# Retention and a gated FFN in one kernel: gates by seven products in tile 2, a relative state, whole-array products and a new order

## The chip, the cores and the metric

The kernel runs on one core of a Trainium2 chip. A core has five engines that run their own instruction streams and meet through semaphores: TensorE (PE, with its weight loads shown apart as PEld), VectorE (DVE), ScalarE (ACT), GpSimd (POOL) and SyncE (SP), which only issues transfers. TensorE writes into PSUM, which has eight banks of 128 x 512 float32; DVE and ACT read them, POOL does not. The metric is the device time of one execution in microseconds (us), as a median of several.

## The reference

```python
def _attn_ref(q, k, v):                     # 4 batches, 8 heads, 768 tokens, 64 wide
    gamma = 1.0 - 2.0 ** (-5.0 - np.arange(H))
    for t in range(S):
        state = gamma * state + einsum('bhd,bhe->bhde', k[:, :, t], v[:, :, t])
        y[:, :, t] = scale * einsum('bhd,bhde->bhe', q[:, :, t], state)

def _moe_ref(x, w_gate, w_val, w_out):      # 3072 tokens, 512 wide, 1536 hidden
    gate = 1.0 / (1.0 + np.exp(-(x @ w_gate)))
    val = x @ w_val
    return gate * val @ w_out
```

The output y of the first part, with the heads side by side, is x of the second. Inputs and output are float32 in memory; the kernel multiplies in bfloat16.

## The kernel before

**Tiles.** The 768 tokens are cut into six chunks of 128. A tile t is one chunk of all four batches: 512 tokens of the FFN. Its attention is done in two "pairs" P = 2t, 2t + 1 of two batches c each. Attention is chunked: scores of a chunk with itself (`scores`, L216) are masked with the decay (`mask`, L221) and multiplied by v (`intra`, L239); what came before enters through a state per head: `inter` (L233) multiplies q by the block-diagonal copy `zbd` of the state, `state` (L261) makes k v of the chunk, with k scaled by the decay (`scaled`, L206 or L209), `state_sum` (L270) adds it to `za`, and `state_out` (L274) copies `za` into `zbd`. `y_out` (L254) scales y by a table `taby` and leaves it transposed in `xT`.

The decay is handled absolutely: k of tile t is divided by gamma to the power of its own token number, and y of tile t is multiplied by gamma to the power of that number. So each tile t > 0 has its own two masks (`tile_tables`, L152, on POOL) and its own table for y (L157, on POOL), and the state is a plain sum.

**FFN.** Gates and values are products of `xT` with `wg` and `wv`, in twelve blocks of 128 hidden units. Direct blocks are made by `up` (512 columns a matmul) or `up_half` (256). Others go by a scheme of seven products in place of eight (`half_product`) on two blocks of units and two halves of the tokens, which needs sums of weights (`halves_sums`, L340, into `ws`) and of inputs (`x_sums`, L350, into `xs`), made once, and evictions with additions afterwards: `gate_copy`, `gate_add`, `gate_sigmoid` (L409, L414, L419) for gates, `val_copy`, `val_add`, `val_finish` (L388, L393, L399 to L404) for values. A direct gate block is one sigmoid (`up_sigmoid`, L308), a direct value block one product of it with the gate (`up_finish`, L311). The output product goes the same way (`product`, with `hidden_sums`, L453, and `weight_sums`, L435), then `fast_copy`, `fast_add` (L489, L494) and `fast_store`. `halves_sums` and `hidden_sums` can be done on DVE or on POOL.

In tile 2 the values go by seven products and the gates are direct; in tiles 3 and 4 both go by seven, in tile 5 both but the gates of the first two blocks.

**Matmuls.** `mm` (L282 to L288) issues a product either whole (L284, a 128 x 128 stationary operand) or as two column halves of 64 (L288), by the flag `whole`. Scores use half the rows and all columns (64 x 128). All results of TensorE but the state's go to one pool `ff` of seven PSUM banks, one bank a call of `bank`. A new tenant of a bank waits until DVE or ACT has read the old one.

**Order.** After a prologue that fills the pipeline and issues the loads of weights and of the first pairs, everything is issued from a list `ORDER` of six strings (L662 to L733), one for each tile, on a manual schedule: each engine runs its instructions in the order in which the strings name the steps. A step is two letters and a number: `gm`, `vm` direct gate and value products, `sg`, `mu` their evictions, `ag` to `bm` the same by halves, `gp`, `gc`, `ga`, `gs` the gate's seven-product steps, `vp`, `vc`, `va`, `vf`, `vd` the value's (vd: finish on DVE), `dp`, `dc`, `da`, `ds` the output's, `ad`, `dd` weight sums on DVE and `aw`, `dw` on POOL, `hs` hidden sums on DVE and `hg` on POOL, `xs`, `xg` input sums, `wp`, `wc` output weights, `tt` tables, `kt`, `sc`, `mk`, `in`, `ia`, `yo`, `sm`, `zs`, `zo` the attention, `lk`, `lq`, `lv` loads of k, q and v issued by POOL, and `xk`, `xq` transposing loads issued by SP. A + or - moves the step to the next or the last tile. A step in capitals sets `whole`; the order before has none.

Of the kernel before, what the change touches and what calls it, by code (L numbers as in the profile page):

```python
# [17 lines left out]
def kernel(  # L18
# [14 lines left out]
    C = 128  # L33
# [17 lines left out]


# [7 lines left out]
    def load(P, *what):  # L60
        for n in what:
            held, x = {"k": (kn, k), "q": (qn, q), "v": (vn, v)}[n]
            held[P] = ld.tile([C, 2 * H, D], BF16, tag=n, name=n + "n", bufs=4)
            nc.gpsimd.dma_start(out=held[P], in_=src(x, P))

    def load_one(P, c, *what):
        for n in what:
            held, x = {"k": (kn, k), "q": (qn, q), "v": (vn, v)}[n]
            if P not in held:
                held[P] = ld.tile([C, 2 * H, D], BF16, tag=n, name=n + "n", bufs=4)  # L70
# [24 lines left out]
    for n, x, eng in (("k", k, nc.sync), ("q", q, nc.sync)):  # L95
        raw[n] = ffn.tile([C, H, D], F32, tag="ob", name="raw", bufs=4)
        eng.dma_start(out=raw[n], in_=x[0, :, 0:C, :].rearrange("h s d -> s h d"))
    early = ffn.tile([128, 4, 128], F32, tag="gs", name="early", bufs=6)
# [24 lines left out]
    nc.vector.tensor_scalar(toky, dist, tok[:, 0:1], None, op0=ALU.add)  # L123
    nc.vector.tensor_tensor(dist, dist, past, op=ALU.add)
    first = const.tile([128, NT], F32, name="first")
    nc.vector.tensor_scalar(first, tok, tok[:, 0:1], None, op0=ALU.subtract)
    mask0 = at.tile([128, 2, NP, C], F32, tag="maskd", name="mask0")
# [5 lines left out]
    tabk = const.tile([128, NT, H], F32, name="tabk")  # L133
    tabz = const.tile([128, NT, NP], F32, name="tabz")
    taby0 = const.tile([128, NP, C], F32, name="taby0")
    maskd, taby = {}, {}
# [11 lines left out]
    def tile_tables(t, i):  # L148
        if i < 2:
            if t not in maskd:  # L150
                maskd[t] = at.tile([128, 2, NP, C], F32, tag="maskd", name="maskd")
            nc.gpsimd.affine_select(maskd[t][:, i], tabk[:, t, i:H:2].unsqueeze(2).to_broadcast([128, NP, C]),  # L152
                                    pattern=[[0, NP], [1, C]], base=0, channel_multiplier=-1,
                                    compare_op=ALU.is_ge, fill=0.0)
            return
        taby[t] = at.tile([128, NP, C], F32, tag="taby", name="taby", bufs=1)
        nc.gpsimd.tensor_tensor(taby[t], taby0, tabz[:, t, :].unsqueeze(2).to_broadcast([128, NP, C]), op=ALU.mult)  # L157
# [5 lines left out]
    def bank(shape, dt=F32):  # L163
        return pf.tile(shape, dt, tag="ff", name="ff", padded_shape=[128, 2 * NP, C] if dt == BF16 else None)

    def new_qkT(P):
        qkT[P] = ld.tile([128, 2, 2, NP, C], BF16, tag="qkT", name="qkT", bufs=4)
# [32 lines left out]
    def scaled(P, h):  # L200
        x = kn[P].rearrange("s (c h) d -> s c h d", c=2)
        if P not in kt:
            kt[P] = ld.tile([C, 2 * H, D], BF16, tag="kt", name="kt", bufs=2)
        to = kt[P].rearrange("s (c h) d -> s c h d", c=2)
        if P < 4:
            nc.vector.tensor_tensor(to, x, tabk[:, P // 2, :].unsqueeze(1).unsqueeze(3).to_broadcast([C, 2, H, D]),  # L206
                                    op=ALU.mult)
        else:
            nc.scalar.activation(to[:, :, h, :], x[:, :, h, :], AX.Copy, scale=tabk[:, P // 2, h:h + 1])  # L209
# [9 lines left out]
    def mask(P, c, i):  # L219
        st[P, c, i] = at.tile([128, NP, C], BF16, tag="st", name="st", bufs=8)  # L220
        nc.vector.tensor_tensor(st[P, c, i], sc[P, c][i], (mask0 if P < 2 else maskd[P // 2])[:, i], op=ALU.mult)  # L221
# [5 lines left out]
    def inter(P, c):  # L227
        y[P, c] = bank([128, NP, C])
        if P > 1:
            for p in range(NP):  # L230
                for i in range(2):
                    half = slice(i * D, (i + 1) * D)
                    nc.tensor.matmul(y[P, c][half, p, :], zbd[P % 2][:, c, p, half], qkT[P][:, 1, c, p, :],  # L233
                                     start=(p == 0), stop=False, skip_group_check=True)
# [7 lines left out]
    def y_out(P, c, eng="a"):  # L242
        t = P // 2
        if t not in xT:
            xT[t] = at.tile([128, NP, 512], BF16, tag="xT", name="xT")
# [7 lines left out]
        else:  # L253
            nc.vector.tensor_tensor(o, y[P, c], taby[t], op=ALU.mult)  # L254
# [9 lines left out]
    def state_sum(P):  # L264
# [4 lines left out]
        else:  # L269
            nc.vector.tensor_tensor(za[j], za[j], zz[P], op=ALU.add)  # L270
# [11 lines left out]
    def mm(during, o, left, right, **kw):  # L282
# [9 lines left out]
    def hidden(t):  # L292
        if t not in hT:
            hT[t] = ffn.tile([128, NFF, 512], BF16, tag="hT", name="hT", bufs=2)
        return hT[t]

    def up(t, n1, which, lo=0, hi=512):
# [3 lines left out]
        for kk in range(KT):  # L301
            mm(t, us[t, n1, which][:, lo:hi], w[:, kk, n1 * 128:(n1 + 1) * 128], xT[t][:, kk, lo:hi],
               start=(kk == 0), stop=(kk == KT - 1))

    def up_sigmoid(t, n1, lo=0, hi=512):
        if (t, n1) not in gated:
            gated[t, n1] = ffn.tile([128, 512], F32, tag="gs", name="gs", bufs=6)
# [5 lines left out]
    def up_half(t, n1, half, which):  # L313
# [3 lines left out]
        for i in range(2):  # L317
            for kk in range(KT):
                mm(t, u[:, i], w[:, kk, (n1 + i) * 128:(n1 + i + 1) * 128], xT[t][:, kk, lo:lo + 256],
                   start=(kk == 0), stop=(kk == KT - 1))  # L320

    def half_sigmoid(t, n1, half):
        gated[t, n1, half] = ffn.tile([128, 2, 256], F32, tag="gs", name="gs", bufs=6)
# [30 lines left out]
    def sigmoids(t, n1):  # L354
        if (t, n1) not in gated:
            gated[t, n1] = ffn.tile([128, 512], F32, tag="gs", name="gs", bufs=6)
        return gated[t, n1]

    def half_product(t, g, n, which):
# [9 lines left out]
        for kk in range(KT // 2):  # L369
# [12 lines left out]
            mm(t, to, left, right, start=(kk == 0 and opens), stop=(kk == KT // 2 - 1))  # L382

    def val_copy(t, g, n):
        if (t, g) not in vals:
            vals[t, g] = ffn.tile([128, 3, 256], F32, tag="scr", name="scr", bufs=2)
# [383 lines left out]
```

## Time and profile before

| | us |
|---|---|
| median of 3 runs | 221.76 (221.68 to 225.01) |
| the profiled execution, device time | 221.94 |
| its span, first to last instruction | 220.2 |
| granted TensorE clock, mean over the span | 0.996 |
| first product of the FFN's order (L288) | at 19.19 |
| last product ends | at 215.9 |

The profile is of one execution. For each engine it lists its instructions with start and length. "Busy" is the time in which at least one instruction of the engine ran; matmuls are pipelined and their lengths modelled, so how fast TensorE really goes is read from the distance of starts. In a row of groups stand the source line, the engine, the operation, what it writes and reads, shapes and count, then total us and mean ns, then the idle time before them with who ended it. "issue" stands where the profile shows nobody.

### The profile page before, as it was taken

To read this page: it belongs to the slowest core of one execution; us is meant where nothing else is said; L and a number is where in the kernel's file an instruction comes from. 1 tells how busy PE (TensorE), PEld (TensorE's weight loads), DVE (VectorE), ACT (ScalarE), POOL (GpSimd) and SP (SyncE) were. 2 spreads that over 40 slices of the span, in tenths; PEclk is the share of its full clock that TensorE was granted. 3 is DMA by queue.
4 is the path that set the end of the run, shared out by engine and by line. 5 is a ranking of instruction groups with operands and counts; after the bars stand their busy time and mean duration, and the time that the engine had idled before them with its cause. 6 is when DMAs were issued, how large, how long until landed. Compare 5 with 4: busy or idle time off the path is not lost. (4 is left out here: it accounts for less than half of the span.)

```text
span 220.2 us, 8636 instructions
## 1 busy us (share of the span) xinstructions
PE 206.8 (94%) x3686; PEld 183.9 (84%) x3686; DVE 183.6 (83%) x367; ACT 140.8 (64%) x371; POOL 162.0 (74%) x169
## 2 busy tenths in 40 slices
PE   6778998998989999999999999999999999999992
PEld 6565555797979979798889989999999899999991
DVE  6577689999877998989999899999988798677750
ACT  7474446254965385993578776986588757868621
POOL 8967786679599748759575999987437766888840
PEclk9999999999999999999999999999999999999998
DMA  9999999999990999929995699977004000002214
GB/s 129 135 171 195 194 175 159 193 190 157 149 121 14 71 149 200 196 63 139 224 191 90 84 110 140 117 215 51 7 36 157 3 4 3 0 3 98 101 57 138
DMA packets 104008, 25.48 MB, mean 116 GB/s; under 512 B 93984, under 2 KB 101152, under 8 KB 103968
## 3 DMA queue, kind: packets, MB, share of 16 engines
q0 software_dynamic: 81248, 13.90, 81.6%
q1 hardware_dynamic: 22576, 10.88, 25.0%
q8 instruction: 29, 0.48, 0.9%
q10 hardware_dynamic: 144, 0.13, 0.2%
q14 instruction: 11, 0.09, 0.1%
HBM read 28.31 MB, written 6.29 MB: 157 GB/s over the span
## 5 line engine op out<-in xcount | busy, mean ns | idle before, releaser
L288 PE MATMUL ff<-xT,wg 128*64 128x256 bf16 (+1 forms) x528 | 49.3, 313 | 0.7 <-DVE st L221 0.7
L288 PEld LDWEIGHTS <-wg 128*64 128x64 bf16 x664 | 36.9, 110 | 8.6 <-issue 1.1
L288 PEld LDWEIGHTS <-wv 128*64 128x64 bf16 x664 | 36.8, 110 | 6.7 <-issue 2.4
L288 PE MATMUL ff<-xT,wv 128*64 128x256 bf16 (+1 forms) x472 | 40.0, 293 | 1.6 <-issue 1.0
L399 POOL TENSOR_TENSOR hT<-gs,scr 128x512 bf16<-128x512 f32 x21 | 27.5, 1315 | 10.6 <-ACT gs L419 4.1
L288 PEld LDWEIGHTS <-hT 128*64 128x64 bf16 x576 | 31.7, 110 | 1.3 <-issue 0.4
L489 ACT COPY ob<-ff 128x256 f32<-128x256 f32 x48 | 17.2, 373 | 21.4 <-PE ff L288 18.7
L288 PE MATMUL ff<-xs,ws 128*64 128x256 bf16 x328 | 30.4, 273 | 0.2 <-ACT scr L388 0.2
L388 ACT COPY scr<-ff 128x256 f32<-128x256 f32 x72 | 25.5, 376 | 7.9 <-PE ff L288 4.5
L288 PEld LDWEIGHTS <-ws 128*64 128x64 bf16 x492 | 27.7, 110 | 1.5 <-issue 0.4
L288 PE MATMUL ff<-wo,hT 128*64 128x256 bf16 x432 | 28.4, 273 | 0.2 <-DVE ob L494 0.2
L393 DVE TENSOR_TENSOR scr<-scr,ff 128x512 f32<-128x512 f32 (+1 forms) x48 | 25.9, 549 | 2.7 <-PE ff L288 2.0
L221 DVE TENSOR_TENSOR st<-ff,maskd 128x512 bf16<-128x512 f32 x40 | 25.7, 683 | 1.2 <-PE ff L216 1.2
L308 ACT ACTIVATE gs<-ff 128x512 f32<-128x512 f32 (+1 forms) x27 | 15.6, 581 | 14.7 <-PE ff L288 13.5
L288 PEld LDWEIGHTS <-hs 128*64 128x64 bf16 x432 | 23.9, 110 | 0.6 <-DVE hs L453 0.3
L414 DVE TENSOR_TENSOR gs<-gs,ff 128x512 f32<-128x512 f32 (+1 forms) x34 | 18.3, 550 | 5.0 <-PE ff L288 2.0
L409 ACT COPY gs<-ff 128x256 f32<-128x256 f32 x51 | 18.1, 376 | 5.0 <-PE ff L288 3.1
L288 PE MATMUL ff<-wt,hs 128*64 128x256 bf16 x288 | 19.4, 273 | 0.0
L209 ACT ACTIVATE kt<-kn,tabk 128x128 bf16<-128x128 bf16 x48 | 17.5, 399 | 2.1 <-issue 2.0
L288 PE MATMUL ff<-xs,wv 128*64 128x256 bf16 x192 | 18.2, 273 | 0.0
L402 POOL TENSOR_TENSOR hT<-gs,scr 128x256 bf16<-128x256 f32 x18 | 13.1, 734 | 6.4 <-ACT gs L409 2.3
L419 ACT ACTIVATE gs<-gs 128x512 f32<-128x512 f32 (+1 forms) x34 | 17.5, 528 | 0.3
(107 smaller groups left out, 429.8 us busy)
## 6 DMA issues: line engine op xcount, KB each, us to landing
out_dram<-ob SPq DMA_DIRECT2D x22, 256.0 KB, 3.8
vn<-in_v_dram POOLq DMA_DIRECT2D x12, 256.0 KB, 7.7
kn<-in_k_dram POOLq DMA_DIRECT2D x11, 256.0 KB, 6.3
qn<-in_q_dram POOLq DMA_DIRECT2D x11, 256.0 KB, 7.4
wo<-in_moe_w_out_dram POOLq DMA_DIRECT2D x4, 384.0 KB, 13.0
wg<-in_moe_w_gate_dram POOLq DMA_DIRECT2D x5, 256.0 KB, 9.4
wv<-in_moe_w_val_dram POOLq DMA_DIRECT2D x5, 256.0 KB, 9.9
out_dram<-ob SPq DMA_DIRECT2D x3, 128.0 KB, 3.3
```

The source lines that it names most:

```text
L209: nc.scalar.activation(to[:, :, h, :], x[:, :, h, :], AX.Copy, scale=tabk[:, P // 2, h:h + 1])
L221: nc.vector.tensor_tensor(st[P, c, i], sc[P, c][i], (mask0 if P < 2 else maskd[P // 2])[:, i], op=ALU.mult)
L288: nc.tensor.matmul(o[half], left[:, half], right, skip_group_check=True, **kw)
L308: nc.scalar.activation(gated[t, n1][:, lo:hi], us[t, n1, 0][:, lo:hi], AX.Sigmoid)
L388: nc.scalar.copy(vals[t, g][:, {1: 0, 5: 2, 3: 1}[n]], m[False][:, 256:] if n == 1 else m[True][:, :256])
L393: nc.vector.tensor_tensor(o, o, x, op=ALU.add)
L399: eng.tensor_tensor(h[:, 2 * g], s, vals[t, g][:, 0:2].rearrange("p two n -> p (two n)"), op=ALU.mult)
L402: eng.tensor_tensor(h[:, 2 * g + 1, 256:], s[:, 256:], vals[t, g][:, 2], op=ALU.mult)
L409: nc.scalar.copy(o, pairs[t, g, 0][x][:, :256] if x else pairs[t, g, 0][x][:, 256:])
L414: nc.vector.tensor_tensor(o, o, pairs[t, g, 0][False][:, cols], op=ALU.add)
L419: nc.scalar.activation(o, x, AX.Sigmoid)
L489: nc.scalar.copy(o, fast[t, i][x][:, :256] if x else fast[t, i][x][:, 256:])
```

## The change

1. **Tile 2.** The steps `gp`, `gc`, `ga`, `gs` (gates by seven products) and `vm`, `mu` (values direct) stand where `vp`, `vc`, `va`, `vf`, `vd` and `gm`, `sg` stood. In tile 5 the gates of blocks 0 and 1 go by seven as well.
2. **Relative state.** Decay is counted within the chunk. One pair of masks for all tiles but the first, one table for y, k scaled by the distance to the chunk's end; the state is multiplied by gamma to the power of 128 when a chunk is added. That multiplication is part of `state_sum`, which is now four instructions, one for each pair of heads. The step `tt` is gone.
3. **Whole array.** Some steps of the order are in capitals (5 in the string of tile 0, 33 in tile 1, 3 in tile 2, and all products but a few at the start of tile 5), among them `IN`, since `inter` now goes through `mm`.
4. **Fixed slots.** Each buffer of a pool is given by a digit of a list `PLACES`, in the order of the calls, PSUM banks too.
5. **New order.** All six strings are new. Weight sums: 27 on DVE and 21 on POOL (38 and 10 before); hidden sums: 42 and 30 (47 and 25 before).

```diff
+    PLACES = {
+        "k": "012310230132",
...
+        "ff": (
+            "012345601230465102346523105426310563104213546231026136013035123065426032540360435104365103165340"
...
+    taken = {}
+
+    def place(pool, shape, dt, tag, name, **kw):
+        n = taken[tag] = taken.get(tag, -1) + 1
+        return pool.tile(shape, dt, tag=tag + PLACES[tag][n], name=name, bufs=1, **kw)
...
-    tok = const.tile([128, NT], F32, name="tok")
-    nc.gpsimd.iota(tok, pattern=[[C, NT]], base=0, channel_multiplier=1, allow_small_or_imprecise_dtypes=True)
+    tok = const.tile([128, 2], F32, name="tok")
+    nc.gpsimd.iota(tok, pattern=[[C, 2]], base=-C, channel_multiplier=1, allow_small_or_imprecise_dtypes=True)
...
-        for p in range(NP):
-            nc.scalar.activation(tabz[:, :, p], first, AX.Exp, scale=lgp[:, p:p + 1])
+        nc.scalar.activation(tabz, lgp, AX.Exp, scale=float(C))
...
-    def tile_tables(t, i):
-        if i < 2:
...
-            nc.gpsimd.affine_select(maskd[t][:, i], tabk[:, t, i:H:2].unsqueeze(2).to_broadcast([128, NP, C]),
...
-        taby[t] = at.tile([128, NP, C], F32, tag="taby", name="taby", bufs=1)
-        nc.gpsimd.tensor_tensor(taby[t], taby0, tabz[:, t, :].unsqueeze(2).to_broadcast([128, NP, C]), op=ALU.mult)
+    def tile_mask(i):
+        nc.gpsimd.affine_select(maskd[:, i], tabk[:, 1, i:H:2].unsqueeze(2).to_broadcast([128, NP, C]),
...
     def bank(shape, dt=F32):
-        return pf.tile(shape, dt, tag="ff", name="ff", padded_shape=[128, 2 * NP, C] if dt == BF16 else None)
+        return place(pf, shape, dt, tag="ff", name="ff", padded_shape=[128, 2 * NP, C] if dt == BF16 else None)
...
-            nc.scalar.activation(to[:, :, h, :], x[:, :, h, :], AX.Copy, scale=tabk[:, P // 2, h:h + 1])
+            nc.scalar.activation(to[:, :, h, :], x[:, :, h, :], AX.Copy, scale=tabk[:, 0, h:h + 1])
...
-                for i in range(2):
-                    half = slice(i * D, (i + 1) * D)
-                    nc.tensor.matmul(y[P, c][half, p, :], zbd[P % 2][:, c, p, half], qkT[P][:, 1, c, p, :],
-                                     start=(p == 0), stop=False, skip_group_check=True)
+                mm(y[P, c][:, p, :], zbd[P % 2][:, c, p, :], qkT[P][:, 1, c, p, :], start=(p == 0), stop=False)
...
-            nc.vector.tensor_tensor(o, y[P, c], taby[t], op=ALU.mult)
+            nc.vector.tensor_tensor(o, y[P, c], taby0, op=ALU.mult)
...
-            nc.vector.tensor_tensor(za[j], za[j], zz[P], op=ALU.add)
+            for p in range(NP):
+                nc.vector.scalar_tensor_tensor(za[j][:, :, p], za[j][:, :, p], tabz[:, p:p + 1], zz[P][:, :, p],
+                                               op0=ALU.mult, op1=ALU.add)
...
-    for i in range(3):
-        tile_tables(1, i)
+    for i in range(2):
+        tile_mask(i)
...
-        "dd0++ dd1++ ad0+ kt0 dd4++ wp1+ gm1 sg1 kt8 vm1 ad1+ ad8+ gm3 gm2 sg2 sm0 zs0 zo1 vm3 vm2 mu2 sg3 ad3+  "
...
+        "ad0+ gm1 sg1 vm1 gm2 VM3 wp1+ dd0+ kt8 kt0 sm1 zs1 GM3 sg3 gm4 gm5 sg4 mu1 sg5 dd8+ sm0 ad8+ gm7 sg7  "
...
```

More of the change, by code (lines that the diff above doesn't have):

```diff
@@ L132 @@
         nc.vector.memset(z, 0.0)
-    tabk = const.tile([128, NT, H], F32, name="tabk")
-    tabz = const.tile([128, NT, NP], F32, name="tabz")
+    tabk = const.tile([128, 2, H], F32, name="tabk")
+    tabz = const.tile([128, NP], F32, name="tabz")
     taby0 = const.tile([128, NP, C], F32, name="taby0")
-    maskd, taby = {}, {}
+    maskd = place(at, [128, 2, NP, C], F32, tag="maskd", name="maskd")
     def tables():
@@ L381, in half_product @@
             }[n]()
-            mm(t, to, left, right, start=(kk == 0 and opens), stop=(kk == KT // 2 - 1))
+            mm(to, left, right, start=(kk == 0 and opens), stop=(kk == KT // 2 - 1))
     def val_copy(t, g, n):
         if (t, g) not in vals:
-            vals[t, g] = ffn.tile([128, 3, 256], F32, tag="scr", name="scr", bufs=2)
+            vals[t, g] = place(ffn, [128, 3, 256], F32, tag="scr", name="scr")
         m = pairs[t, g, 1]
@@ L430, in weight_sums @@
         if i in (1, 2):
[L431 removed]
+            sums[g, i] = place(ffn, [128, 3, 256], F32, tag="scr", name="scr")[:, :2]
         o, x, z, op = (lambda: (wt[:, 0, fs], b12, b11, ALU.subtract), lambda: (sums[g, 1], b22, b12, ALU.subtract),
@@ L477, in product @@
             }[n]()
-            mm(t + 1, to, left, right, start=(f == 0 and opens),
+            mm(to, left, right, start=(f == 0 and opens),
                stop=(f == NFF // 2 - 1))
@@ L485, in fast_copy @@
         if (t, i, "o") not in fast:
-            fast[t, i, "o"] = tuple(ffn.tile([128, D_MODEL], F32, tag="ob", name="ob", bufs=4) for _ in range(2))
+            fast[t, i, "o"] = tuple(place(ffn, [128, D_MODEL], F32, tag="ob", name="ob") for _ in range(2))
         lo, hi = fast[t, i, "o"]
```

68 lines of the change are left out of this document (38 added, 30 removed), and 137 rows, old and new, of the table ORDER.

## Prediction

> **What bounds the kernel now.** I read the page first: shares of the engines and the chain that ended last.
>
> ```profile
> span 220.2 us, 8636 instructions
> PE 206.8 (94%) x3686; PEld 183.9 (84%) x3686; DVE 183.6 (83%) x367; ACT 140.8 (64%) x371; POOL 162.0 (74%) x169
> PE 40%; DVE 2%; ACT 1%; POOL 1%; issue 0%; DVEq 0%; ACTq 0%
> ```
>
> The profiled execution took 221.94 us, 1.74 us more than its span; the median of the three runs is 221.76, so the sum below starts from 221.94 and may be read against either. TensorE is busy for 94% and carries the chain. Whether it streams or only overlaps itself is to be read from starts, so next the chain in order of time and the timeline of TensorE (start, length, what, count).
>
> ```profile
> 141.35 0.60 DVE scr L393
> 141.95 0.60 DVE xT L254
> 142.55 0.33 DVE gs L414
> ...
> 177.64 35.21 PE ff L288 x628
> ```
>
> ```profile
> 15.92 0.60 PE L284 MATMUL ff<-xT,wg 128*128 128x256 bf16 x4 [0.94 <-ACT xT L252]
> 16.35 0.60 PE L284 MATMUL ff<-xT,wv 128*128 128x256 bf16 x4
> 16.88 0.30 PE L239 MATMUL ff<-st,vn 128*64 128x128 bf16 x4
> ...
> 126.97 0.41 PE L288 MATMUL ff<-xT,wg 128*64 128x256 bf16 x4
> 127.19 0.41 PE L288 MATMUL ff<-xs,wv 128*64 128x256 bf16 x4
> 127.53 0.40 PE L216 MATMUL ff<-qkT 64*128 64x128 bf16 x8
> 127.86 0.41 PE L288 MATMUL ff<-xs,ws 128*64 128x256 bf16 x4
> ```
>
> A product is issued as two column halves that run together: four halves, two "slots" of 256 columns, from 126.97 to 127.19, so 0.11 us a slot. The last stretch says it finer: 628 halves are 314 slots, eight of them (two direct gate blocks of the last tile) 512 wide, so 322 slots of 256 in 35.21 us, 0.109 us each with nothing lost for 35 us. The whole-array product of the prologue, 15.92 to 16.35 for four, takes 0.108. So both forms stream at one column rate, and TensorE can only gain where it stands still.
>
> Where it stands still is in the list of waits, TensorE alone (total, times, longest):
>
> ```profile
> PE ff L288 <- issue: 1.0, 1, 1.0
> ...
> PE ff L288 <- DVE st L221: 0.7, 1, 0.7
> PE ff L216 <- DVE hT L311: 0.6, 1, 0.6
> ...
> PE ff L288 <- ACT gs L419: 0.5, 1, 0.5
> PE ff L233 <- DVE xT L254: 0.2, 1, 0.2
> PE ff L288 <- ACT scr L388: 0.2, 1, 0.2
> PE ff L288 <- DVE ob L494: 0.2, 1, 0.2
> ```
>
> (The rows left out lie in the first 19 us, whose code hardly changes.) Read who ended them: scores (L216) do not use hT, products (L288) do not use st, scr or ob. Six of the seven are waits for a PSUM bank that DVE or ACT had not yet emptied; the seventh names nobody. They idle for 3.4 us; a matmul's modelled length reaches over the next start, so each also hides a drain:
>
> ```profile
> L288 PEld LDWEIGHTS <-hT 128*64 128x64 bf16 x576 | 31.7, 110 | 1.3 <-issue 0.4
> L288 PE MATMUL ff<-wo,hT 128*64 128x256 bf16 x432 | 28.4, 273 | 0.2 <-DVE ob L494 0.2
> L399 POOL TENSOR_TENSOR hT<-gs,scr 128x512 bf16<-128x512 f32 x21 | 27.5, 1315 | 10.6 <-ACT gs L419 4.1 <-DVE scr L393 3.5 <-ACT gs L409 2.1
> L402 POOL TENSOR_TENSOR hT<-gs,scr 128x256 bf16<-128x256 f32 x18 | 13.1, 734 | 6.4 <-ACT gs L409 2.3 <-ACT gs L419 2.1 <-DVE xT L254 0.8
> L404 DVE TENSOR_TENSOR hT<-gs,ff 128x256 bf16<-128x256 f32 x24 | 9.7, 415 | 1.8 <-PE ff L288 1.5 <-ACT gs L409 0.2
> L311 DVE TENSOR_TENSOR hT<-gs,ff 128x512 bf16<-128x512 f32 x11 | 7.4, 681 | 2.1 <-PE ff L288 2.1
> L152 POOL TENSOR_SCALAR_AFFINE_SELECT maskd<-tabk 128x512 f32<-128x512 f32 x10 | 6.7, 679 | 1.2 <-DVE st L221 1.2
> L453 DVE TENSOR_TENSOR hs<-hs,hT 128x512 bf16<-128x512 bf16 x10 | 5.9, 595 | 0.1
> L270 DVE TENSOR_TENSOR za<-za,z 128x512 f32<-128x512 f32 x8 | 5.5, 682 | 0.3 <-ACT ob L489 0.2
> L157 POOL TENSOR_TENSOR taby<-taby,tabz 128x512 f32<-128x512 f32 x5 | 5.2, 1034 | 0.0
> L206 DVE TENSOR_TENSOR kt<-kn,tabk 128x1024 bf16<-128x1024 bf16 x4 | 4.9, 1218 | 0.0
> L453 DVE TENSOR_TENSOR hs<-hT 128x512 bf16<-128x512 bf16 x11 | 4.6, 422 | 1.2 <-POOL hT L402 1.0
> L340 DVE TENSOR_TENSOR ws<-ws,wg 128x256 bf16<-128x256 bf16 x6 | 3.7, 613 | 0.0
> L340 POOL TENSOR_TENSOR ws<-wg,ws 128x256 bf16<-128x256 bf16 x3 | 2.1, 698 | 0.2 <-DVE ws L340 0.2
> L340 DVE TENSOR_TENSOR ws<-wg,ws 128x256 bf16<-128x256 bf16 x3 | 0.8, 283 | 0.0
> L284 PEld LDWEIGHTS <-wv 128*128 128x128 bf16 x8 | 0.8, 97 | 0.1
> ```
>
> 273 ns against a slot of 109: 0.164 each, 1.1 for seven. All bank waits together cost 3.4 + 1.1 = **4.5 us**. That is nearly all that any new order can win.
>
> What makes DVE late is also in these groups (the numbers are total us and mean ns): equal sums cost 422 or 595, 283 or 613. Here is one such case, DVE and TensorE in one place:
>
> ```profile
> 49.46 1.26 DVE L453 TENSOR_TENSOR hs<-hs,hT 128x512 bf16<-128x512 bf16 x1
> 50.65 0.68 DVE L221 TENSOR_TENSOR st<-ff,maskd 128x512 bf16<-128x512 f32 x1
> ...
> 51.38 1.06 PE L288 MATMUL ff<-xT,wg 128*64 128x256 bf16 x16 [0.70 <-DVE st L221]
> ```
>
> A sum from two SBUF operands took 1.26 us instead of 0.42, the mask behind it emptied its bank late, and TensorE stood. SBUF sums are the ops that stretch; over the thirty ops of the four quoted DVE sum groups the excess is (10 x 0.173 + 6 x 0.330) / 30 = 0.12 us each. I take POOL's own work at the same time for the cause, as it is the only other engine here with such operands. The page "SBUF — State Buffer" of the Trainium skill (Who interferes with whom) says so too: a DVE instruction with two SBUF inputs and a GpSimd one that reads SBUF exclude each other. The lengths above agree.
>
> **The change part by part.**
>
> *Gates instead of values by seven products, tile 2.* TensorE: the same 42 seven-product steps and 12 direct blocks; in the last tile the gates of block pair 0 also go by seven, 14 slots for 16: -0.2 us. DVE per pair: the two additions stay (on gates instead of values); two direct products of 681 take the place of one of 415: +0.95, six pairs +5.7; three finishes that DVE did for POOL in this tile go, about -1.8 (681, 681 and 415). POOL loses the other nine, four of 1315 and five of 734: -8.9. ACT gets six more, and three in the last tile, at 140.8/371 = 0.4 us: +3.4 of an engine at 64%, hidden.
>
> *Who makes the sums.* Counting the new order's steps: weight sums on DVE 38 to 27, on POOL 10 to 21; hidden sums on DVE 47 to 42, on POOL 25 to 30. DVE -11 x 0.283 - 5 x 0.422 = -5.2; POOL +11 x 0.698 + 5 x 1.2 = +13.7 (1.2: a POOL op of 512 elements, from the nearest rows 1034 and 1315).
>
> *Relative state.* POOL loses five tables of 1034 and eight of ten masks of 679: -10.6, and the wait of a mask for its predecessor's readers. DVE: each of eight state sums (682) becomes four of 128 elements with a scale. No row shows that instruction; 415 at 256 and 681 at 512 extrapolate to 0.28, so +0.45 each, +3.6; bounds: 0 (four quarters of 682) and four of 415, +7.8. I take 3.6, since both rows also read PSUM. ACT's state_out waits for four instead of one; up to 0.45 us on an engine with a third of its time free. L233 may be whole, the same count of slots.
>
> DVE in all: +5.7 - 1.8 - 5.2 + 3.6 + 1.1 (two gate additions in the last tile) = +3.4; two-operand SBUF ops fall from 106 to 88, -18 x 0.12 = -2.2. Net +1.2 of 183.6. POOL: -8.9 + 13.7 - 10.6 = -5.8. Totals hardly move; places do.
>
> *Whole array.* 536 slots of 256 and 24 of 512 become whole. By the rows 0.109 against 0.108: -0.3 us over 560 slots, no more. But a change of array shape costs: from L288 at 127.19 to L216 at 127.53 are 0.34 for two slots, 0.12 over; L216's four slots of 128 columns (0.055 each) take 0.33, 0.11 over; and from whole to halves, 16.35 to 16.88 for four slots, 0.09 over. In the order of instructions such changes behind the prologue go from 27 to 42. Entering the whole form without a wait is in no row: bounds 0 and 0.12. Fifteen more at 0 to 0.12 are 0 to 1.8; as half of them are of the kind not seen I take 0.05: +0.8.
>
> A rule of the Trainium skill speaks against this part: "TensorE: Matmul & The Clock Gate" (Part 3, The mechanism) has a weight load overlap a running matmul only in other row groups, which a whole-array load never has. It becomes a rival below.
>
> *Fixed slots and order.* The same seven banks, now handed out by a list. I set matmul slots as a clock along both orders and looked when a bank's last product ended and its next tenant began: within 1 us of streaming in 38 of 239 cases before, 63 after, in the last tile 4 against 13. A tight one needs a drain and an ACT copy in between, so I allow 0.1 us for each of the 25 new: +2.5 if all show. Against this, the old bank waits can go: -4.5. Between these ends I take the middle, **-1.0**. Of the steps that move, the 18 loads that POOL issues in the order stand behind fewer masks and tables; the stores and transposing loads on SP keep their sequence but for places, and SP is no engine in the chain: 0, and if such a load is late, the scores behind it wait.
>
> Sum: 221.94 - 0.2 - 0.3 + 0.8 - 1.0 = **221.2 us**.
>
> **The rivals.**
>
> *All bank waits go (B).* For: six of seven are bank waits and the list of banks is what was rewritten; POOL, which stretches DVE, has 5.8 us less. Against: the tighter hand-overs. 221.94 - 0.5 - 4.5 + 0 to 0.8 = 216.9 to 217.7.
>
> *DVE becomes the bound in the second string of the order (C), slower.* That string now has 39 DVE ops of 512 elements at the spacing 0.60 that the chain shows (0.08 under their length), 11 sums at 0.34, 9 at 0.20, two state sums of 4 x 0.20 and one L206 at 1.14: 31.6 us. TensorE has 266 slots at 0.109, 104 of 128 columns at 0.055 and 24 half as long: 35.4. The room, 3.8 us over its 20 SBUF sums, decides: above 0.19 us of stretch each, TensorE waits; the mean was 0.12. POOL's steps in this string, counted alike, rise from 13.9 to 19.5 us. At 0.5 each it is 20 x 0.5 - 3.8 = 6.2 us: 227.4. Against: in the third string before, 34 sums had a like room, (37.9 - 31.8) / 34 = 0.18 each when counted the same way, and TensorE still lost only the few waits listed above.
>
> *Whole-array loads lie in the open (D).* 560 times 0.097: 276 us. The trace speaks against it: L284 has a new weight for each product, loads 97 ns, and still starts one every 0.108 us. By that rule the time is 276; the trace does not bear it out.
>
> *Whole-array loads were the limit (E):* 560 x (110 - 97) ns = 7.3 us less, 214.6. Against: slots of halves pass at 0.109, which no 13 ns of load moved. The same page (Weight-path perf modes) gives fast loads to 128-column weights alone, which would be this gain.
>
> **How the numbers follow.** About 2% (4.4 us) can be told from no change. Forecast 0.55 (219 to 224); B 0.20, half of it under 217.3; C 0.20, nine tenths of it over 226.2; D 0.01, E 0.02; 0.02 for something slower that I do not see. Faster 0.10 + 0.02 = 0.12; slower 0.18 + 0.01 + 0.02 = 0.21; within 0.67. The range reaches from just under B, 216.5, to C's price, 227.5.
>
> **What would show it.** In the new profile: slots at 0.109 or 0.108 in both forms (else D or E); about 42 changes of shape at 0.1 or less; the rows that TensorE waits for, their sum near 3.5 us with drains, naming ff readers (B: near nothing; C: several us between 40 and 80, behind DVE); four state sums of some 0.28 us; L453 and L340 on DVE nearer to 422 and 283. The forecast is wrong if TensorE waits for data, a load or a transposed qkT, in place of a bank.

## The result, and the profile after

The changed kernel takes **231.62 us** as the median of four executions (226.80, 229.24, 234.01 and 235.99); the kernel before took 221.72 on the same chip. The ratio is 1.033 (95% interval 1.025 to 1.040): slower. A second set of four gave 1.039 (1.033 to 1.046). The forecast was 221.2, its range ended at 227.5. Executions of the changed kernel lie further apart than those before; ratios and the "kept" times below leave out those more than 1.5% above the fastest of the same kernel, and of the kernel before on the same chip, and "others" are those left out.

The profiled execution of the changed kernel took 234.01 us, so it is one of the two long ones; profiles of kept executions come with the experiments. The page of it, the engines' shares:

```profile
span 232.3 us, 7525 instructions
PE 212.2 (91%) x3130; PEld 179.9 (77%) x3130; DVE 193.8 (83%) x380; ACT 143.3 (62%) x378; POOL 154.5 (67%) x162
```

POOL lost 7.5 us (forecast 5.8), DVE gained 10.2 (forecast 1.2). What TensorE waited for most after 20 us (total, times, longest):

```profile
PE ff L302 <- DVE ob L508: 4.9, 3, 2.8
PE ff L302 <- DVE st L236: 1.5, 1, 1.5
PE ff L231 <- DVE hT L325: 1.3, 1, 1.3
```

These are PSUM banks that DVE emptied late, as before, but the longest is 2.8 us against 0.7, and all waits after 20 us come to 9.2 us against 3.4. Here is the longest, from the timelines (start, length) of TensorE, then DVE, then POOL:

```profile
86.69 0.39 PE L302 MATMUL ff<-xT,wg 128*64 128x256 bf16 x4
87.00 0.39 PE L298 MATMUL ff<-xT,wg 128*128 128x256 bf16 x2
...
87.45 0.82 PE L298 MATMUL ff<-wo,hT 128*128 128x256 bf16 x6
88.20 0.41 PE L302 MATMUL ff<-xs,ws 128*64 128x256 bf16 x4
...
88.69 0.39 PE L302 MATMUL ff<-xs,ws 128*64 128x256 bf16 x4
91.88 0.85 PE L302 MATMUL ff<-wt,hT 128*64 128x256 bf16 x12 [2.79 <-DVE ob L508]
```

```profile
85.22 0.67 DVE L508 TENSOR_TENSOR ob<-ob,ff 128x512 f32<-128x512 f32 x1
85.82 5.67 DVE L467 TENSOR_TENSOR hs<-hT 128x512 bf16<-128x512 bf16 x2
91.42 0.41 DVE L508 TENSOR_TENSOR ob<-ob,ff 128x256 f32<-128x256 f32 x1
```

```profile
83.15 1.15 POOL L88 DMA_DIRECT2D vn<-in_v_dram  x1
84.31 2.13 POOL L354 TENSOR_TENSOR wg<-wg 128x256 bf16<-128x256 bf16 x3
86.41 1.32 POOL L364 TENSOR_TENSOR xs<-xT,xs 128x512 bf16<-128x512 bf16 x1
87.70 1.15 POOL L467 TENSOR_TENSOR hs<-hs,hT 128x512 bf16<-128x512 bf16 x1
88.81 0.66 POOL L354 TENSOR_TENSOR ws<-ws,wv 128x256 bf16<-128x256 bf16 x1
89.44 0.66 POOL L354 TENSOR_TENSOR wg<-wg 128x256 bf16<-128x256 bf16 x1
90.07 1.14 POOL L467 TENSOR_TENSOR hs<-hT,hs 128x512 bf16<-128x512 bf16 x1
91.57 1.15 POOL L467 TENSOR_TENSOR hs<-hs,hT 128x512 bf16<-128x512 bf16 x1 [0.36 <-DVE hs L467]
```

Read the three together. POOL issued loads until 84.31 and then ran eight sums without a pause until 91.21. DVE came to two hidden sums at 85.82 that take 0.42 us each alone. The first takes 0.91 and ends at 86.73, behind the first three of POOL's sums (84.31 to 86.45). The second starts at 86.65 and stands for 4.84 us, until the run is over: 5.67 us for the two. POOL's next sum needs its result, which is why the run ends there (the last line). The addition behind them in DVE's queue empties the bank that TensorE's next product needs, and TensorE stands for 2.79 us. I call this a **hold**. A group's mean hides it: fifteen such sums have a median of 420 ns and a longest of 4839:

```profile
L467 DVE TENSOR_TENSOR hs<-hT x15: 409/420/4839, 33.6 to 220.2; 128x512 bf16<-128x512 bf16 x15
```

And the wait costs more than its length. A stretch of this execution, with the granted clock as the third number from the right:

```profile
92.00:97.00 5.00, 4.09 (x40) 3.31 (x39) 3.85 (x9) 1.97 (x6) 0.72 (x1) 0.69 0.63 167
```

After the wait the clock, 1.00 before, is down to 0.69 over 5 us (0.50 from 93.9 to 97.3), so the products behind it run slower too.

The rest went as the rows before had said. From the chain, 80 halves at 160 us and 290 whole products in the last string, and the group of the state sums:

```profile
160.22 4.38 PE ff L302 x80
193.31 32.05 PE ff L298 x290
L283 DVE SCALAR_TENSOR_TENSOR za<-za,tabz,z 128x128 f32<-128x128 f32 x32 | 8.9, 339 | 0.0
```

4.38 / 40 and 32.05 / 290 are 0.110 and 0.111 us a slot: both forms stream. A change of shape costs 0.31 - 0.22 = 0.09 into the whole form (86.69 to 87.00) and 0.75 - 0.65 = 0.10 out of it (87.45 to 88.20). The last row is the state sum: 339 ns for a quarter, and four in a row take 1.11 us (those that start at 82.61).

### The profile page after: what moved, and what is told of

Its sections match the earlier page's. It is cut to its first block, busy times and chain, and to the rows that moved or that the text cites. A ratio compares the mean times of both kernels' runs of the same rounds, so it can differ in the third digit from the quotient of the medians.

```text
span 232.3 us, 7525 instructions
## 1 busy us (share of the span) xinstructions
PE 212.2 (91%) x3130; PEld 179.9 (77%) x3130; DVE 193.8 (83%) x380; ACT 143.3 (62%) x378; POOL 154.5 (67%) x162
## 3 DMA queue, kind: packets, MB, share of 16 engines
HBM read 28.31 MB, written 6.29 MB: 149 GB/s over the span
## 4 chain that ended last, share of the span: by engine, by line
PE 82%; DVE 9%; DMA 3%; issue 2%; ACT 2%; POOL 1%; DVEq 0%; POOLq 0%
PE ff L302 48%; PE ff L298 27%; PE ff L231 3%; PE ff L251 3%; DMA kn<-in_k_dram 3%; DVE ws L354 2%; DVE ob L508 1%; PE z L273 1%; DVE za L283 1%; DVE hT L325 1%; DVE hs L467 1%; ACT taby L167 1%; PE ff L193 1%; DVE xT L266 1%; DVE kt L221 0%
## 5 line engine op out<-in xcount | busy, mean ns | idle before, releaser
L302 PE MATMUL ff<-xT,wv 128*64 128x512 bf16 (+1 forms) x296 | 32.5, 344 | 0.0
L302 PEld LDWEIGHTS <-wv 128*64 128x64 bf16 x392 | 24.4, 114 | 6.1 <-issue 1.1
L302 PEld LDWEIGHTS <-wg 128*64 128x64 bf16 x396 | 23.0, 113 | 5.9 <-issue 2.1
L302 PE MATMUL ff<-xT,wg 128*64 128x256 bf16 (+1 forms) x252 | 24.4, 310 | 1.5 <-DVE st L236 1.5
L302 PEld LDWEIGHTS <-hT 128*64 128x64 bf16 x336 | 18.9, 111 | 6.9 <-issue 5.4
L325 DVE TENSOR_TENSOR hT<-gs,ff 128x512 bf16<-128x512 f32 (+1 forms) x25 | 16.0, 659 | 6.3 <-PE ff L302 4.4
L298 PE MATMUL ff<-xT,wg 128*128 128x256 bf16 (+1 forms) x118 | 17.7, 288 | 1.6 <-ACT xT L264 0.7
L298 PE MATMUL ff<-xT,wv 128*128 128x256 bf16 (+1 forms) x120 | 18.0, 288 | 0.0
L298 PEld LDWEIGHTS <-wg 128*128 128x128 bf16 x142 | 13.6, 98 | 5.2 <-issue 2.0
L302 PE MATMUL ff<-wo,hT 128*64 128x256 bf16 x240 | 15.8, 273 | 1.5 <-DVE ob L508 1.2
```

Source lines behind the costliest of these rows:

```text
L298: nc.tensor.matmul(o, left, right, skip_group_check=True, **kw)
L302: nc.tensor.matmul(o[half], left[:, half], right, skip_group_check=True, **kw)
L325: nc.vector.tensor_tensor(hidden(t)[:, n1, lo:hi], gated[t, n1][:, lo:hi], us[t, n1, 1][:, lo:hi], op=ALU.mult)
```

## The experiments

P is the theory that DVE's sums of two SBUF operands are held while POOL runs sums back to back. L is the rival that DVE is simply full.

**One part at a time.** Four runs on one chip. First, all products in halves again (every capital in the order made small):

```diff
-        "... gm2 VM3 wp1+ ... GM3 sg3 ..."
+        "... gm2 vm3 wp1+ ... gm3 sg3 ..."
```

> The changed kernel with every step of the order issued as column halves again (no capitals), all else as changed. Theory P (DVE's sums of two SBUF operands are blocked behind a backlog of POOL's, late DVE leaves PSUM banks full, TensorE stands): whole arrays have no part in it, so the time stays within 1.5 us of the changed kernel, about 227 to 230, and the long waits for DVE in the strings of tiles 1 and 2 remain. Theory W (whole arrays cost: 15 more changes of array shape, or weight loads in the open): 2 us or more faster, down to 222 if it is the whole loss. Slots of 256 columns at 0.109 us either way.

Measured: ratio 1.020 (1.016 to 1.025), kept 225.3 to 226.4. P had 227 to 230 and missed; a gain of 2 us or more is what W expected. But the wait of 2.8 us is gone from its profile too, and the longest sum took 3.11 us, so this run can't tell the whole array from where the holds fall. Second, the sixteen weight sums that POOL does in the second and third strings given to DVE (`aw`, `dw` to `ad`, `dd`):

> The changed kernel with the 16 weight sums that POOL makes in the strings of tiles 1 and 2 given back to DVE, at the same places. Theory P: POOL loses 16 x 0.68 = 11 us of work where DVE was blocked; the excess of DVE's two-operand sums falls from 22 us to under 14, the wait of 2.8 us near 89 us goes and with it the second half-clock stretch: 3 to 7 us faster than the changed kernel, 222 to 226. Theory O (the order or the slots as such make TensorE wait): no gain, or up to 3 us slower, since DVE has 16 x 0.28 = 4.5 us more to do.

Measured: 1.021 (1.015 to 1.027), kept 225.4 and 227.0 (others 230.7 and 233.7), where P had 222 to 226; the wait of 2.8 us is gone from its profile. Third, the relative state put into the kernel before, nothing else (`tile_mask`, one `taby`, the state sum in four, no `tt`):

> The kernel before with the relative state alone: one pair of masks, one table for y, state sums of four instructions; the table steps leave the order, nothing else moves. Theory P: POOL loses 10.6 us, DVE gains 8 x (1.11 - 0.68) = 3.4 us, so this part alone is a small change: 219 to 223. A theory that blames the four-part state sums (R): 3 us or more slower than before, 225 or above.

Measured: 1.007 (1.004 to 1.011), 1.6 us, kept 221.9 to 224.5 (others 225.4 and 226.5). Fourth, the changed kernel with its buffers taken in turn, without the list:

```diff
-        n = taken[tag] = taken.get(tag, -1) + 1
-        return pool.tile(shape, dt, tag=tag + PLACES[tag][n], name=name, bufs=1, **kw)
+        n = len(set("".join(PLACES[tag])))
+        return pool.tile(shape, dt, tag=tag, name=name, bufs=n, **kw)
```

> The changed kernel with buffers taken from rotating pools again, of the same sizes, in place of the fixed digits. Theory P: the slots are not the cause; within 2 us of the changed kernel or slower, since the order was laid out for these slots: 226 to 232. Theory S (fixed slots hand a bank on too early in the order, so TensorE waits for its reader): 2 us or more faster, 222 to 226.

Measured: 1.022 (1.017 to 1.027), kept 226.3 and 226.7 (others 236.0 and 237.7), with the same waits for `ob`: the fixed slots show no effect of their own. Each of the first two takes a part away, and several us remain.

**Where the holds fall.** The changed kernel once more:

> The changed kernel, unaltered, as the neighbour of the next two runs and for a trace at full clock. All theories: 226.5 to 227.5 us where nothing disturbs it, some 5 us over the kernel before. Theory P (VectorE's sums of two SBUF operands are held up while GpSimd runs sums back to back) expects the held pair at about 86 us again, over 4 us for two sums that take 0.84 alone, and TensorE waiting over 2 us for the ob addition behind it. Rival J (that pair was an accident of one execution): no such pair, and the 5 us are spread over many waits under 1 us.

Measured: 1.039, kept 229.0 to 230.2 (another 235.9, the profiled one), above the 226.5 to 227.5 that all theories had. The pair was held again, 5.67 us at 88.38, and the profile has a worse one. DVE, then POOL, then TensorE:

```profile
49.74 8.26 DVE L354 TENSOR_TENSOR ws<-ws,wg 128x256 bf16<-128x256 bf16 x1
57.92 1.27 DVE L266 TENSOR_TENSOR xT<-ff,taby 128x512 bf16<-128x512 f32 x2
```

```profile
49.41 1.15 POOL L449 TENSOR_TENSOR scr<-scr,wo 128x512 f32<-128x512 f32 x1
50.52 1.14 POOL L449 TENSOR_TENSOR wt<-wo 128x512 bf16<-128x512 bf16 x1
...
56.71 1.14 POOL L449 TENSOR_TENSOR scr<-wo 128x512 f32<-128x512 bf16 x1
```

```profile
59.25 1.87 PE L298 MATMUL ff<-xT,wg 128*128 128x256 bf16 x8 [6.29 <-DVE xT L266]
60.91 1.91 PE L298 MATMUL ff<-xT,wv 128*128 128x256 bf16 x8
```

A sum that takes 0.28 us stood for 8.26, until POOL's run ended at 57.85. TensorE stood for 6.29, and its next eight products took 1.66 us, 0.208 each, twice the usual. In this kernel's first profile the same sum took 2.7 us.

On the same chip, the held pair handed to POOL (`hs0- hs8-` to `hg0- hg8-`):

> The changed kernel with only the two hidden sums that stood for 5.7 us in its trace (first sums of block groups 0 and 2 of tile 1) done by GpSimd in place of VectorE. GpSimd then has 2 x 1.15 us more at its fullest place. Theory P: the ob addition behind them comes in time, the wait of 2.8 us goes, 2 to 3 us less than the changed kernel. Rival L (VectorE is simply full there, whoever is delayed): what VectorE gains, the next addition loses to its own sums; under 0.7 us gained. Rival Q (GpSimd, two sums later, delays what reads the sums): 0 to 2 us slower.

Measured: 1.057 (1.051 to 1.063), kept 233.4 to 234.1 (another 237.4, the profiled one): Q, and 2 us more than Q allowed. What P says of the pair comes true, and the remedy is wrong:

```profile
85.28 1.02 DVE L508 TENSOR_TENSOR ob<-ob,ff 128x512 f32<-128x512 f32 x2
86.22 0.35 DVE L354 TENSOR_TENSOR ws<-ws,wv 128x256 bf16<-128x256 bf16 x1
91.10 0.69 DVE L428 TENSOR_TENSOR gs<-gs,ff 128x512 f32<-128x512 f32 x1 [4.54 <-PE ff L302]
```

DVE's additions come in time and DVE then idles for 4.5 us, which speaks against L here. But the first of the two sums made POOL wait 4.25 us for DVE's data, all behind it came late, and TensorE's waits now name POOL, and a hold further on:

```profile
PE ff L298 <- DVE xT L266: 6.3, 1, 6.3
PE ff L302 <- DVE gs L428: 4.3, 1, 4.3
...
PE ff L302 <- POOL xs L364: 1.2, 1, 1.2
```

The 4.3 us stand behind a hidden sum that took 5.95 us from 99.54, in place of the pair. The first row is the weight sum at 50 us again, which stood for 8.23 us, so that hold was no accident of one execution.

Then the state summed in one instruction:

```diff
-            for p in range(NP):
-                nc.vector.scalar_tensor_tensor(za[j][:, :, p], za[j][:, :, p], tabz[:, p:p + 1], zz[P][:, :, p],
-                                               op0=ALU.mult, op1=ALU.add)
+            nc.vector.tensor_tensor(za[j], za[j], zz[P], op=ALU.add)
```

> The changed kernel with the state summed in one instruction, as before, which leaves out the multiplication of the old state by the decay of a chunk. VectorE has 8 x 0.43 = 3.4 us less, with nothing of two SBUF operands among it. If VectorE bounds wherever TensorE stands (rival L): 1.5 to 3 us less than the changed kernel. Theory P (single held sums bound, in a few places): 0.3 to 1.2 us less, as state sums lie near the held places at 82.6 and 94.3 only. The forecast, which hid the 3.6 us: 0.

Measured: 1.012 (1.004 to 1.020), kept 222.8 to 225.2 (another 228.0). That is some 6 us less than the changed kernel on the same chip, more than any of the three expected. In its profile no sum took more than 3.11 us: the one that stood for 8.26 came at the same place in POOL's run and took 1.08. So an edit can change the time through where the holds fall, and this one doesn't yet price the state sum.

And the kernel before with eleven weight sums given to POOL (`ad`, `dd` to `aw`, `dw`, six in the second string and five in the third):

> The kernel before with eleven of VectorE's weight sums in the strings of tiles 1 and 2 handed to GpSimd, as many as the change moved, and nothing else. VectorE loses 11 x 0.283 us, GpSimd gains 11 x 0.7. Theory P: the kernel before has 1 us of pauses between GpSimd's sums there, so sums on VectorE are held longer: excess over 15.3 us by 3 to 6, and 1 to 4 us slower. The forecast's mean stretch (0.12 us for each sum, fewer of them on VectorE): no slower than 0.5 us.

Measured: 1.023 (1.017 to 1.028), kept 224.7 to 227.9, 5 us, with nothing else changed. The profile is of a kept execution (227.45), and one hold carries most of it, here on DVE and on TensorE:

```profile
83.18 5.11 DVE L350 TENSOR_TENSOR xs<-xT 128x512 bf16<-128x512 bf16 x1
```

```profile
88.94 0.41 PE L288 MATMUL ff<-xs,wv 128*64 128x256 bf16 x4 [3.18 <-DVE scr L393]
```

Behind this wait the granted clock was 0.50 from 90.2 to 93.6. L had no room here, since DVE lost work. P's mechanism is right and its sizes are not: the excess of all such sums rose by some 2 us, where P had 3 to 6, and the time by 5, where it had 1 to 4. Here one place counts, not the total.

**Moving the sums, or opening the run.** Two reorderings. In the second string, DVE's sums out of POOL's run of 47 to 58 us:

```diff
-  hs4- hg5- sc7 ... wp5 wp6 ia7 ... AV6 wp7 kt36 dd21 yo7 ... hs8- zs3 BG4 am6 hs9- am2 hs6- ... hs7- am4 hs11- BV4 bm4 hs2- wc1
+  hs4- dd21 hs6- hg5- sc7 ... wp5 ia7 ... AV6 kt36 yo7 ... zs3 BG4 am6 am2 ... am4 hs7- BV4 bm4 hs2- hs8- hg9- wp6 wp7 wc1
```

(`hs11-` goes behind `am0`.) In the third, two POOL sums that need the held pair put ahead of POOL's other sums, so that POOL must wait for DVE:

```diff
-  lq7- lv7- gc01 ... zo10- hg1- aw9- ... mu3 hg3- hg9- hs4-
+  lq7- lv7- hg1- hg9- gc01 ... zo10- aw9- ... mu3 hg3- hs4-
```

> The changed kernel, with VectorE's sums moved out of the run of GpSimd sums of the second string (47 to 58 us): the weight sum that stood for 8.3 us there and one hidden sum go ahead of the masks, four hidden sums go behind the run, one of them to GpSimd, and two of GpSimd's output weight sums behind that. The engines' work is the same but for one sum. Theory P (sums on VectorE are held for as long as GpSimd runs sums without a pause): no sum held at 50 us, the wait of 6.3 us for xT gone and the half clock behind it too; 4 to 7 us less than the changed kernel run in the same place as its neighbour last (229 to 230), so 223 to 226. Rival L (VectorE is full): the same sums delay something else, under 1 us gained. Rival C' (the half clock comes by itself and the hold is only its company): the half clock stays.

> The changed kernel, with only the third string touched: two of GpSimd's hidden sums, which need VectorE's held pair, stand ahead of GpSimd's three weight sums and an input sum, so that GpSimd has to pause until the pair is done. No work is added or taken away. Theory P: the pair takes 0.8 to 2 us in place of 5.7, the wait of 2.8 us behind it goes, and if the hold of the second string stays as it is, 2 to 4 us less than the changed kernel. Rival L: under 0.7. Rival Q (GpSimd is then late with the input sums and TensorE waits for those): 0 to 2 us slower.

> Both reorderings together. Theory P: near the sum of the two, 221 to 224 us, VectorE's excess over undisturbed sums from 22 us down to 16 or less, no half clock between 20 us and the end. Rival L: 227 us or more.

> Both reorderings, and all products of the order in halves again. With the holds gone this prices the whole array by itself. By the forecast (0.3 us gained in slots, 15 more changes of shape at 0 to 0.12 us): 0 to 1 us less than with both reorderings alone. If the whole array itself brings the clock down (rival C'): 2 us less or more.

Measured, in this order:

- The second string: 1.032 (1.022 to 1.042), kept 227.7 and 229.1 (others 234.4 and 238.1).
- The third string: 1.001 (0.995 to 1.007), kept 220.0 to 223.0; but these are four of ten, and the others took 224.05 to 230.72.
- Both: 1.031 (1.021 to 1.041), kept 227.7 to 229.4 (another 235.6).
- Both in halves: 1.006 (1.001 to 1.010), kept 221.2 to 222.7, six of ten; the others took 237.0 to 241.4.

The first misses P's 223 to 226: in its profile a hidden sum ahead of the masks took 2.63 us, and TensorE stood 4.4 us for a mask. In the third string's profile (224.13 us) the pair takes 0.75 and no sum is held at 50 us, so its kept executions are level with the kernel before, better than P expected; none of its executions at 228 to 231 was profiled. In both together a hold has moved on to the next sum in the queue. DVE and POOL of that run, a kept execution:

```profile
78.35 0.75 DVE L467 TENSOR_TENSOR hs<-hT 128x512 bf16<-128x512 bf16 x2
79.02 0.41 DVE L508 TENSOR_TENSOR ob<-ob,ff 128x256 f32<-128x256 f32 x1
79.35 7.56 DVE L354 TENSOR_TENSOR ws<-ws,wv 128x256 bf16<-128x256 bf16 x1
```

```profile
79.15 2.29 POOL L467 TENSOR_TENSOR hs<-hs,hT 128x512 bf16<-128x512 bf16 x2
...
85.62 1.14 POOL L467 TENSOR_TENSOR hs<-hT,hs 128x512 bf16<-128x512 bf16 x1
```

The pair is free now; the weight sum behind it waits 7.56 us for POOL's nine sums. P was right on the single hold and wrong that moving two of them suffices. The last run therefore can't price the whole array: its neighbour has this hold in a kept execution, and it has it itself in a long one (8.20 us in its profile, 237.16 us).

So the run itself was opened: behind each POOL sum one POOL instruction of another kind, that writes two zeros per partition into a tile nobody reads.

```diff
+    def gap(eng):
+        if eng is nc.gpsimd:
+            nc.gpsimd.memset(gone, 0.0)
...
         eng.tensor_tensor(o, x, z, op=op)
+        gap(eng)
```

> The changed kernel with one more GpSimd instruction behind each of its sums: a write of two zeros for each partition into a tile that nobody reads, so GpSimd's runs of sums have a gap after each sum. Estimated at 0.1 to 0.2 us each (its copy of two elements takes 0.19), it adds work for GpSimd and takes none from VectorE. Theory P (a sum on VectorE is held as long as GpSimd's sums follow each other without a gap): no hold over 1.4 us, 220 to 224 us, and executions agree within 2 us. Rival L (VectorE is full): no change, 227 to 231. Rival S (any GpSimd instruction holds, or the gap is too short): holds of 4 us and more stay, 227 to 233.

> The kernel before with the same gap behind each GpSimd sum. Its longest hold was 1.7 us. Theory P: between 1 us less and 1 us more than without, 220 to 222.

> The changed kernel with the gaps and all products of the order in halves. If the whole array costs by itself (rival C'): 1.5 us or more under the kernel with gaps alone. Theory P: within 1 us of it.

> The gaps together with the reordering of the third string (GpSimd's two dependent hidden sums ahead of its other sums). Theory P: the executions at 228 to 231 us that the reordered kernel had are gone, 219.5 to 222.5 us. Rival S: they stay.

Measured:

- Gaps alone: 223.7 and 224.2 kept, but 229.7 and 229.8 in the other two, so the executions do not agree within 2 us.
- Gaps in the kernel before: 1.000 (0.996 to 1.004).
- Gaps and halves: 1.013 (1.009 to 1.018), kept 223.8 to 224.8. That is within 1 us of gaps alone, so the whole array costs nothing here.
- Gaps and the third string reordered: 1.008 (1.005 to 1.011), kept 221.8 to 222.7, eight of ten. Another took 229.0, so P's "gone" is too strong, and one took 539.9, which nothing here explains.

The place of the 8.26 us hold, in the kernel with gaps alone:

```profile
50.10 2.75 DVE L360 TENSOR_TENSOR ws<-ws,wg 128x256 bf16<-128x256 bf16 x1
```

```profile
49.74 1.15 POOL L457 TENSOR_TENSOR scr<-scr,wo 128x512 f32<-128x512 f32 x1
50.84 0.09 POOL L349 MEMSET gone<- 128x2 bf16 x1
50.90 1.14 POOL L457 TENSOR_TENSOR wt<-wo 128x512 bf16<-128x512 bf16 x1
51.98 0.09 POOL L349 MEMSET gone<- 128x2 bf16 x1
52.04 0.66 POOL L360 TENSOR_TENSOR ws<-wv 128x256 bf16<-128x256 bf16 x1
```

POOL's run still goes on to 58.8, but DVE's sum gets through behind the third POOL sum that it meets (the last line), not at the first. My bound of 1.4 us for a hold was too tight. In the profile of the last of the four the same sum took 1.41. One place proves little, as this sum took 1.08 us in a kernel without gaps. Over all traces, the longest sum of the changed kernel and its variants is 2.63 to 8.26 us in the eleven without gaps and 1.54 to 3.78 in the five with them. So the gap shortens holds, as far as these traces go, and doesn't rule them out.

**The rest of 2 us.** With gaps and the reordered third string, once with one-instruction state sums and once in halves:

> The kernel with gaps and the reordered third string, with the state summed in one instruction (which leaves out the multiplication of the old state by the decay of a chunk): VectorE has 3.4 us less. The relative state alone had cost the kernel before 0.7% (1.6 us). If that is the rest of 2 us: 220.3 to 221.2 us. If VectorE's total no longer matters once no sum is held: 222 us.

> The kernel with gaps and the reordered third string, with all products of the order in halves. By the forecast's terms (0.3 us more in slots, up to 1.8 us less in changes of shape): between 1 us less and 0.3 us more than with whole products, 221.3 to 222.6 us. If the whole array is the rest of 2 us: 220.3.

Measured: 1.005 (1.002 to 1.008), kept 220.7 to 222.2 (another 227.6); and 1.015 (1.009 to 1.020), kept 222.1 to 224.8. The state sum is some 0.6 us of the 1.8, though the intervals overlap; the whole array is no loss, halves are if anything slower. About 1 us isn't assigned: the new order, or the gaps' own time. The execution of 227.6 was profiled, and it has a hold in spite of the gaps; the masks behind it came late and TensorE stood for 4.02 us:

```profile
49.21 3.78 DVE L358 TENSOR_TENSOR ws<-ws,wg 128x256 bf16<-128x256 bf16 x1
```

## Why the prediction was wrong

**Streams and shapes: right.** Both forms run at 0.110 to 0.111 us a slot, so the rivals D (276 us) and E (214.6) are out. The rule of the Trainium skill behind D ("TensorE: Matmul & The Clock Gate", Part 3, The mechanism) was not borne out, as the rows of before had said. A change of shape costs 0.09 to 0.10, and entering the whole form is no exception; I took +0.5 us for the whole array, and in the kernel with gaps halves gain nothing.

**POOL's total: nearly right. DVE's: not.** POOL fell by 7.5 for 5.8. The state sum takes 1.1 for four, as forecast (4 x 0.28), but the sum gave the relative state no term, and alone it costs the kernel before 1.6 us. DVE rose by 10.2 for 1.2, and nearly all of the 9.0 between is stretch: what its sums of two SBUF operands take beyond their undisturbed length was to fall by 2.2 us, and it rose by nearly 7, from 15 to 22. TensorE's waits were to stay near 3.5 us, for banks as before; they are for banks, and came to 9.2.

**Fixed slots and order, -1.0: the sign.** Of the bounds -4.5 to +2.5, what is left when the holds are mostly gone is +1.8 for everything together, not -0.7.

**The step that failed is the price of a stretched sum.** I wrote that "SBUF sums are the ops that stretch" and then "the excess is ... 0.12 us each". That mean I multiplied by a number of operations, so eighteen fewer on DVE came out as 2.2 us gained. The cause was right and named: POOL's own work at the same time. But a held sum does not always wait for one POOL sum: it can wait for the rest of a run of them. How long that can be is set by how many POOL sums follow each other without a pause, and the change lets POOL do eleven weight sums and five hidden sums more. In the first profile they stand in runs of eleven (46.84 to 58.05) and eight, and DVE starts its own sums inside. The kernel before has a run of ten (58.94 to 69.70), but DVE starts a single such sum in it, and that one got through after 1.12 us. The page "SBUF — State Buffer" of the Trainium skill (Who interferes with whom) has an exclusive lock for a whole instruction; the runs agree on the exclusion, and show that it can go to the same engine seven times in a row (the POOL sums that start from 50.52 to 56.71).

**Rival C had the right place and the wrong test.** It said that DVE becomes the bound in the second string, at 0.20. Its point of decision was an average, 3.8 us of room over 20 sums. A hold needs no such room to be used up: an instruction right behind it empties a bank, and TensorE needs that bank within some 2 us (holds of 4.84, 5.11, 7.56 and 8.26 us made it wait 2.79, 3.18, 5.31 and 6.29). DVE idles elsewhere in the string, so the room is there and can't be used. A mean of 0.5 us a sum gave C 227.4, and the kept executions took 226.8 to 230.2; that the two are close is luck, as single holds of 5 to 8 us made the loss.

**What was not seen at all** is that a wait can bring the clock down. The longest wait in the profile of before after the prologue is 1.03 us, so it could not show it.

The kernel before with eleven sums moved (1.023) shows that moving sums to POOL is enough for 5 us, the larger part of the loss (1.033 and 1.039). That the holds are the way it comes about is seen in its trace, and fits the gaps with the third string (229 to 230 down to 222.3 in eight of ten); since these are two edits, and each alone leaves long executions, neither is shown to be the cure. Giving sixteen sums back to DVE took away only a part (1.021), and what else its order costs is open.

What decides in one execution whether a sum slips in between two POOL sums is not settled either. Few are held: in the first profile four of DVE's 81 sums of weights, inputs and hidden values took more than 1.9 us. At the same place in the same run one took 1.08 us in one kernel and 8.26 in another, and the third string's edit, which lies behind 80 us, can't be why the hold at 50 us was small in its profile. Nor are POOL's sums the only thing that holds: in the kernel before, a weight sum that takes 0.28 us alone took 1.30 from 86.08, while POOL issued a load (85.97 to 87.19), and the hold of 5.11 us ended at 88.29, in a load's issue behind POOL's run. No version beat the kernel before.

## What to carry to other kernels

Before giving sums from VectorE to GpSimd to relieve it, look in the timeline for GpSimd's runs without a pause, and for VectorE's sums of two SBUF operands that start inside them: such a sum can cost the rest of the run, so a share of a mean doesn't price it. Look at minimum, median and longest of such a group, and at the instruction queued behind the longest. If the runs can't be avoided, a short GpSimd instruction of another kind after each sum can be tried: here the longest hold with it was 3.78 us against 8.26, and it cost the kernel before nothing (1.000). Take several executions, since one order had some at 220 us and some at 231.

## What the hardware showed unexpectedly

The granted clock fell to half after TensorE had stood for 2.8 us (0.69 over the 5 us from 92) and around a wait of 6.3 us (this stretch, of the second profile, has most of it):

```profile
59.00:67.00 8.00, 7.75 (x46) 5.89 (x46) 5.47 (x14) 1.87 (x5) 0.00 (x0) 0.62 0.99 111
```

"TensorE: Matmul & The Clock Gate" of the Trainium skill (Part 1) has the clock halve after an idle window of about 3.4 us. The 2.8 us wait is shorter, but products ran for only 1.1 us before the next wait, of 0.9 us, and 3.7 us of the 4.8 from 89.09 to 93.85 were idle. The first profile has a shorter case still: 0.50 from 52.9 to 56.3, after waits of 1.33 and 1.51 us within 4.4 us. In the changed kernel with the state summed in one instruction, waits of 1.23 and 1.94 us (up to 82.73 and 85.74) passed at full clock, 1.00 from 82 to 93. So the length of a single wait doesn't decide it; what does, these runs don't show.
